# Weights in groups of two tiles, and one bank of G masked straight from PSUM, in a fused SSD and ReGLU kernel

## The chip, the cores and the metric

The kernel runs on one core of a Trainium2 chip. The metric is the device time of one execution in microseconds (us); of several runs the median is taken. Below, PE is the matrix engine (TensorE), DVE is VectorE, ACT is ScalarE, POOL is GpSimd and SP is the engine that issues most loads.

## What is computed

A state-space layer (SSD, in chunks) is followed by a gated feed-forward layer over the same tokens. Cut to what matters:

```python
# x: 4 x 8 x 768 x 32, a: 4 x 8 x 768, B and C: 4 x 8 x 768 x 16; for each chunk:
    L = np.exp(cum[:, :, :, None] - cum[:, :, None, :]) * causal
    CB = np.einsum('bhin,bhjn->bhij', Cc, Bc)
    y_intra = np.einsum('bhij,bhjd->bhid', CB * L, xc)
    y_inter = np.einsum('bhin,bhnd->bhid', Cc, state) * decay_to_i[:, :, :, None]
    y[:, :, sl] = y_intra + y_inter
    state = decay_full[:, :, None, None] * state + np.sum(Bx, axis=2)
# then, with the heads put side by side: 3072 tokens x 256
    gate = np.maximum(x @ w_gate, 0.0)      # w_gate, w_val: 256 x 1536
    val = x @ w_val
    return gate * val @ w_out               # w_out: 1536 x 256
```

## The kernel before

**Tiling.** The state-space layer goes over pairs of 128 positions: 12 pairs of 256 tokens, three for each of four batches. The feed-forward layer goes over six blocks of 512 tokens (two pairs each). Its inner width of 1536 is cut into 12 tiles of 128, called f. For each f, a gate and a value product are formed in PSUM (`gv` for 512 tokens, lines 589 to 601; `gvh` for one pair of 256, lines 603 to 623), ScalarE applies the ReLU, VectorE multiplies, and the result lies in `h` in SBUF. When all 12 tiles of a block are there, `fout` (line 625) multiplies `h` by `wo`, 12 matmuls for each 128 tokens.

**Weights.** `wg`, `wv` and `wo` hold the three weight matrices in bf16 for the whole run. The inputs are in float32, and GpSimd's DMA queue casts them on the way (`weights`, line 186, and `weights_out`, line 192). One `weights(f0, f1)` is two DMAs, one for `wg` and one for `wv`, each of 256 rows. `weights_out` is one DMA of 12 x 128 rows. All of them go through one queue (q0 in the profile) in the order in which GpSimd issues them, and GpSimd also computes between them. The loads of x, B and C are issued by SP (q1), the first few by ScalarE too (q10).

**One pair in the first batch.** For pairs 0 to 2, B and C are scaled by running products of `a` (`scale_wide`, line 269; factors in `wfac`), transposed by TensorE (`turn`, line 657, k=1 for C and k=0 for B) and copied out of PSUM with a mask (`tevac`, line 323). `G_wide` (line 365) forms the products of B and C in four PSUM banks, q = 0 to 3. Each bank is brought to SBUF as bf16 (`gs`) and masked causally. This is done in one of two ways: `gcopy` (line 387) copies with ScalarE and `gmask` (line 381) then masks in SBUF; or `gmask(..., True)` reads PSUM and masks in the same instruction. `adds` (line 397) forms the state's increments from the scaled B and the cast x (`cast_x`, line 299); `carry` and `pass_on` (lines 420 and 431) run the state on; `inter_wide` and `D_wide` (lines 438 and 454) form y; `yevac_wide` (line 468) writes it to `yT`, which the feed-forward layer reads. `decay` (line 240) forms factors for the later batches from `cp` and `pick`; `pick` is finished by GpSimd in `middle` (line 234), once VectorE has `rmid`.

**Order.** The order on each engine is that of the program text: `in_order` (line 15) chains the instructions of each engine as they were written. The start of the kernel (lines 663 to 800) is written out by hand; the loop from line 802 on does the remaining blocks. `keep_warm(n)` issues n matmuls whose result nobody reads. PSUM tiles called `bank` share five banks in turn, so a product waits until the fifth one before it has been read. The raw loads have four buffers in turn.

**Around the change.** Before it issues the first weights, GpSimd copies one element of `wfac` into a small tile `gate` (line 668), so that the weights' transfers begin only after VectorE has made `wfac` (line 667). Then come `weights(0, 2)` and `weights(2, 6)`, the scaling of pair 1 in four instructions (lines 680 and 681, printed at L277 in the profile), the cast of pair 1 (line 682), `pick`, `weights(6, NF)`, the mask of bank 1 of pair 1 (line 727) and `weights_out` (line 728), and then the scaling of pair 2 (lines 742 and 743).

Of the kernel before, what the change touches and what calls it, by code (L numbers as in the profile page):

```python
# [8 lines left out]
FP32 = mybir.dt.float32  # L9
# [20 lines left out]
def kernel(  # L30
# [13 lines left out]
    nc = tc.nc  # L44
# [7 lines left out]
    NF = DF // 128  # L52
# [4 lines left out]
    const = ctx.enter_context(tc.tile_pool(name="const", bufs=1))  # L57
# [8 lines left out]
    def bank(name="bank", shape=(128, 512), dtype=FP32):  # L66
        return mm.tile(list(shape), dtype, tag="shared", bufs=NSHARED, name=name)
# [109 lines left out]
    def keep_warm(n, rhs=warm):  # L177
        w = bank("w", (128, 128))
        for _ in range(n):
            nc.tensor.matmul(out=w, lhsT=warm, rhs=rhs, start=True, stop=True)  # L180

    wg = glob.tile([128, 2, DF], BF16)
    wv = glob.tile([128, 2, DF], BF16)
    wo = glob.tile([128, NF, DM], BF16)

    def weights(f0, f1):
        fs = slice(f0 * 128, f1 * 128)
        for w, src in ((wg, moe_w_gate), (wv, moe_w_val)):
            nc.gpsimd.dma_start(
                out=w[:, :, fs], in_=src[:, fs].rearrange("(k p) f -> p k f", k=2))  # L190

    def weights_out(f0, f1):
        nc.gpsimd.dma_start(
            out=wo[:, f0:f1, :],
            in_=moe_w_out[f0 * 128:f1 * 128, :].rearrange("(o i) m -> i o m", i=128))

    gate = const.tile([1, 2], FP32)

# [1 line left out]
    wfac = glob.tile([128, 2, 2, NH, PPB], FP32)  # L202
# [37 lines left out]
    def decay():  # L240

        d = mm.tile([128, HC, 2, NB, 8], FP32, tag="tp", name="dec")
        for k in range(HC):
            nc.tensor.matmul(
                out=d[:, k].rearrange("p w b h -> p (w b h)"),
                lhsT=cp[:, k * 128:(k + 1) * 128],
                rhs=pick.rearrange("p w h -> p (w h)"),
                start=(k == 0), stop=True, skip_group_check=True)
        st["dec"] = d
# [19 lines left out]
    def scale_wide(p, j, eng):  # L269
        s = st[p]  # L270
        if "bs" not in s:
            s["bs"] = bs = att.tile([128, 4, 128], BF16, tag="bs", name="bs")
            s["tin"] = [[bs[:, 2 * j + r] for r in range(2)] for j in range(2)]
        src = s["bcr"].rearrange("s (t q) j r n -> s j r t q n", t=2)[:, j]
        f = wfac[:, j, :, :, p]
        for t in range(2):
            eng.tensor_tensor(  # L277
                out=s["bs"][:, 2 * j:2 * j + 2].rearrange(
                    "s k (q t n) -> s k t q n", q=4, t=2)[:, :, t],
                in0=src[:, :, t],  # L280
                in1=f[:, :, 4 * t:4 * t + 4].to_broadcast([128, 2, 4, N]),
                op=ALU.mult)
# [16 lines left out]
    def cast_x(p, ceng):  # L299
        s = st[p]  # L300
        cast = ceng.copy if ceng is nc.scalar else ceng.tensor_copy
        xb = att.tile([128, 2 * NH * D], BF16, tag="xb", name="xb")
        if p < NWIDE:
            cast(xb, s["xr"].rearrange("s h r d -> s (h r d)"))
            s["xb"] = xb.rearrange("s (h r d) -> s h r d", h=NH, r=2)
        else:
            cast(xb, s["xr"].rearrange("s i h d -> s (i h d)"))
            s["x"] = [xb[:, i * NH * D:(i + 1) * NH * D] for i in range(2)]
# [56 lines left out]
    def G_wide(p):  # L365
        s = st[p]
        g = [bank("g%d" % q, (128, 2, 2, 128)) for q in range(4)]
        for r in range(2):
            for i in range(2):
                for q in range(4):  # L370
                    rows = slice(32 * q, 32 * q + 32)
                    nc.tensor.matmul(  # L372
                        out=g[q][64 * i:64 * i + 64, r],
                        lhsT=s["BT"][rows, r, 64 * i:64 * i + 64], rhs=s["CT"][rows, :, i],
                        start=(r == 0), stop=True, tile_position=(32 * q, 64 * i),
                        skip_group_check=True)
        s["gp"] = g
        s["gs"] = att.tile([128, 4, 4, 128], BF16, tag="gs", name="gs", bufs=2)
        s["gw"] = s["gs"].rearrange("s q (r t) m -> s q r t m", r=2)

    def gmask(p, q, eng, psum=False):
        s = st[p]
        d = s["gw"][:, q]
        m = wmask.unsqueeze(2).to_broadcast([128, 2, 2, 128])
        eng.tensor_tensor(out=d, in0=s["gp"][q] if psum else d, in1=m, op=ALU.mult)  # L385

    def gcopy(p, q):
        s = st[p]
        nc.scalar.copy(out=s["gw"][:, q], in_=s["gp"][q])  # L389

    def y_wide(p):
        s = st[p]
        if "yw" not in s:
            s["yw"] = [mm.tile([128, 512], FP32, tag=t, name=t) for t in ("y", "Aps")]
            s["begun"] = [False, False]

    def adds(p):
        y_wide(p)
        s = st[p]
        s["A"] = [s["yw"][i][:, 256:320] for i in range(2)]  # L400
        if p == 0:
            s["A"][0] = bank("A0", (128, 2 * D))
        halves = [i for i in range(2) if 2 * p + i < NC - 1]
        for r in range(2):
            for i in halves:
                half = slice(64 * i, 64 * i + 64)
                for q in range(4):
                    nc.tensor.matmul(
                        out=s["A"][i][32 * q:32 * q + 32],
                        lhsT=s["bs"][half, r, 32 * q:32 * q + 32],  # L410
                        rhs=s["xb"].rearrange("s (t q) r d -> s q r t d", t=2)[half, q, r],
                        start=r == 0, stop=True,
                        tile_position=(64 * i, 32 * q), skip_group_check=True)
        for i in halves:
            s["begun"][i] = p > 0 or i > 0
# [4 lines left out]
    def carry(p, i):  # L420

        c = 2 * p + i
        T_[c] = n = att.tile([128, 2 * D], FP32, tag="T", name="T", bufs=3)
        if c == 0:
            nc.scalar.copy(out=n, in_=st[p]["A"][i])
        else:
            nc.vector.scalar_tensor_tensor(
                out=n, in0=T_.pop(c - 1), scalar=dec[:, c - 1:c], in1=st[p]["A"][i],
                op0=ALU.mult, op1=ALU.add)

    def pass_on(p, i):

        c = 2 * p + i
        S[c + 1] = m = att.tile([128, 2, D], BF16, tag="Sw", name="Sw", bufs=3)
        src = st[p]["A"][i] if c == 0 else T_[c]
        nc.scalar.mul(m.rearrange("s t d -> s (t d)"), src, dec[:, c:c + 1])
# [166 lines left out]
    def gvh(b, f, u, later=False):  # L603

        if f == 0 and u == 0:
            fst[b] = ffn.tile([128, NF, 512], BF16, tag="h", name="h")
        tk = slice(b * 512 + u * 256, b * 512 + (u + 1) * 256)
        fs = slice(f * 128, (f + 1) * 128)
        gv_ = bank("gv", (128, 2, 256))
        for j, w in ((0, wg), (1, wv)):  # L610
            for k in range(2):
                nc.tensor.matmul(out=gv_[:, j], lhsT=w[:, k, fs], rhs=yT[:, k, tk],  # L612
                                 start=(k == 0), stop=(k == 1), skip_group_check=True)
        r = ffn.tile([128, 512], BF16, tag="r", name="r", bufs=5)[:, 0:256]
        nc.scalar.activation(r, gv_[:, 0], AF.Relu)  # L615

        def finish():
            nc.vector.tensor_tensor(out=fst[b][:, f, u * 256:(u + 1) * 256], in0=r,  # L618
                                    in1=gv_[:, 1], op=ALU.mult)

        if later:
            return finish
        finish()
# [37 lines left out]
    V, A_, P_ = nc.vector, nc.scalar, nc.gpsimd  # L661
# [3 lines left out]
    decays(0)  # L665
    keep_warm(8)
    nc.vector.tensor_copy(wfac[:, 1], d)
    nc.gpsimd.tensor_copy(gate[:, 0:1], wfac[0:1, 1, 0, 0, 0:1])
    weights(0, 2)
    weights(2, 6)  # L670
    scale_wide(0, 1, V)
    nc.vector.reciprocal(wfac[:, 0, :, :, 0], wfac[:, 1, :, :, 0])
    scale_wide(0, 0, V)
# [5 lines left out]
    scan(0, H)  # L679
    scale_wide(1, 1, P_)  # L680
    scale_wide(1, 0, P_)
    cast_x(1, P_)
    keep_warm(6)
    G_wide(0)
    keep_warm(7)
# [3 lines left out]
    cast_x(0, A_)  # L689
    decays(1)  # L690
    adds(0)
    gcopy(0, 1)
    gmask(0, 3, V, True)
    keep_warm(4, st[0]["gw"][:, 3, 0, 0])
    gmask(0, 0, V)
    gmask(0, 1, V)
    pass_on(0, 0)
    carry(0, 0)
    middle()
# [6 lines left out]
    load(2)  # L706
    load(3)
    carry(0, 1)
    weights(6, NF)
    tevac(1, V, A_)  # L710
    pass_on(0, 1)
    def halves(b, u, *fs):
# [2 lines left out]

    f0 = gvh(0, 0, 0, True)
    G_wide(1)
    adds(1)
    decay()
    gcopy(1, 0)  # L720
    gmask(1, 2, V, True)
    f0()
# [1 line left out]
    gmask(1, 3, V, True)  # L724
    carry(1, 0)
    pass_on(1, 0)
    gmask(1, 1, P_)
    weights_out(0, NF)
    gmask(1, 0, V)
    late = [gvh(0, f, 0, True) for f in (1, 2, 3)]  # L730
    inter_wide(1)
    D_wide(1)
# [169 lines left out]
```

## Time and profile before

| | |
|---|---|
| median of 5 runs | 128.39 us (127.72 to 129.1) |
| profiled execution | 128.29 us |
| its span, first to last instruction | 126.5 us |
| TensorE matmuls busy | 119.4 us, 94% of the span |
| VectorE, ScalarE, GpSimd busy | 88.4, 81.8 and 42.3 us |
| DMA | 12.15 MB, mean 96 GB/s |
| GpSimd's queue q0 | 3184 packets, 2.36 MB |
| SP's queue q1 | 66096 packets, 8.91 MB |
| `wg` and `wv`, tiles 0 to 1: issue to landing | 5.0 and 4.5 us |
| tiles 2 to 5 | 5.2 and 7.0 us |
| tiles 6 to 11 | 6.7 and 8.0 us |
| `wo` | 11.3 us |
| matmul with 256 or 512 columns | 273 or 379 ns |
| mask from PSUM on VectorE (L385) | 629 to 692 ns |
| mask from SBUF on VectorE (L385) | 426 to 867 ns |
| mask from SBUF on GpSimd (L385) | 1150 to 1156 ns |

Times in the profile are counted from the start of the span. An engine's row gives its start, its duration, and in brackets how long the engine had been idle before and what ended the wait. A weight DMA's "issue" is GpSimd's own time for it, 0.7 to 1.1 us; the transfer runs afterwards, and "to landing" counts from the beginning of the issue until the semaphore says that the data is there.

### The profile page before, as it was taken

The numbers are of one execution on the slowest core, as the hardware profiler recorded it, in microseconds if no ns is written. First come the engines' busy times: TensorE is split into PE (matmuls) and PEld (weight loads), VectorE is DVE, ScalarE is ACT, GpSimd is POOL, SyncE is SP. The second block draws the span as 40 slices with busy tenths as digits, with TensorE's granted clock in tenths as the row PEclk, the third lists the DMA queues.
The fourth block names the chain that finished last, engine by engine and source line by source line (L and its number), as shares of the span: only waits on it lengthen the run. The fifth ranks groups of instructions, "written<-read, shape, count | busy, mean of one in ns | idle before, by whom it ended". The sixth has DMA issues, their size and how long they took to land.

```text
span 126.5 us, 3627 instructions
## 1 busy us (share of the span) xinstructions
PE 119.4 (94%) x1382; PEld 83.5 (66%) x1388; DVE 88.4 (70%) x196; ACT 81.8 (65%) x184; POOL 42.3 (33%) x86
## 2 busy tenths in 40 slices
PE   6979798999999999999999999999999999999980
PEld 6856583378776478875477865577864678844770
DVE  4795887755799675998674898664989656788420
ACT  0478587845688843787936787845987646877310
POOL 6589807418345016802312803232600033000000
PEclk9999999999999999999999999999999999999998
DMA  4999999976997988597922399802200002200031
GB/s 66 210 178 201 173 212 199 123 97 81 113 111 208 112 101 97 152 145 88 108 39 88 89 115 111 105 8 83 88 0 0 0 0 88 83 0 0 5 120 46
DMA packets 72209, 12.15 MB, mean 96 GB/s; under 512 B 65936, under 2 KB 72192, under 8 KB 72192
## 3 DMA queue, kind: packets, MB, share of 16 engines
q1 hardware_dynamic: 66096, 8.91, 46.3%
q0 software_dynamic: 3184, 2.36, 12.5%
q10 hardware_dynamic: 2912, 0.66, 2.5%
q8 instruction: 11, 0.18, 0.6%
q14 instruction: 6, 0.05, 0.2%
HBM read 11.13 MB, written 3.15 MB: 113 GB/s over the span
## 4 chain that ended last, share of the span: by engine, by line
PE 83%; DMA 9%; DVE 2%; ACT 2%; POOL 1%; issue 1%; DVEq 0%; POOLq 0%
PE o L630 26%; PE gv L612 16%; PE val L597 14%; PE gate L594 12%; DMA wo<-in_moe_w_out_dram 9%; PE w L180 3%; PE y L569 2%; PE g L481 2%; PE tp L321 2%; PE y L558 1%; ACT gs L389 1%; PE g L372 1%; POOL gs L385 1%; PE A_ps L528 1%; DVE bs L277 1%
## 5 line engine op out<-in xcount | busy, mean ns | idle before, releaser
L601 DVE TENSOR_TENSOR h<-r,val 128x512 bf16<-128x512 bf16 x44 | 29.5, 686 | 9.2 <-ACT r L600 7.0
L630 PE MATMUL o<-wo,h 128*128 128x256 bf16 x288 | 34.2, 273 | 0.4 <-DMA wo<-in_moe_w_out_dram 0.4
L630 PEld LDWEIGHTS <-h 128*128 128x128 bf16 x288 | 27.1, 98 | 5.6 <-issue 1.5
L600 ACT ACTIVATE r<-gate 128x512 bf16<-128x512 f32 x44 | 25.9, 600 | 6.5 <-PE gate L594 4.5
L597 PE MATMUL val<-yT,wv 128*128 128x512 bf16 x88 | 26.2, 379 | 0.8 <-DMA wv<-in_moe_w_val_dram 0.5
L594 PE MATMUL gate<-yT,wg 128*128 128x512 bf16 x82 | 24.9, 379 | 0.0
L618 DVE TENSOR_TENSOR h<-r,gv 128x256 bf16<-128x256 bf16 x56 | 22.5, 418 | 2.7 <-ACT r L615 1.8
L615 ACT ACTIVATE r<-gv 128x256 bf16<-128x256 f32 x56 | 21.4, 385 | 2.5 <-PE gv L612 0.5
L612 PE MATMUL gv<-yT,wv 128*128 128x256 bf16 x112 | 21.4, 273 | 0.7 <-DMA wv<-in_moe_w_val_dram 0.7
L612 PE MATMUL gv<-yT,wg 128*128 128x256 bf16 x112 | 21.5, 273 | 0.1
L489 POOL TENSOR_SCALAR_AFFINE_SELECT gs<-gs 128x512 bf16<-128x512 bf16 (+1 forms) x18 | 9.0, 523 | 33.0 <-ACT gs L500 33.0
L506 DVE TENSOR_TENSOR gs<-g,maskUT 128x512 bf16<-128x512 f32 x18 | 11.6, 686 | 11.7 <-issue 9.6
L291 POOL TENSOR_TENSOR bs<-bcr,scaleBC 128x256 bf16<-128x256 f32 x18 | 11.0, 633 | 20.0 <-PE val L597 5.8
L597 PEld LDWEIGHTS <-wv 128*128 128x128 bf16 x88 | 8.5, 98 | 10.9 <-DMA wv<-in_moe_w_val_dram 0.8
L594 PEld LDWEIGHTS <-wg 128*128 128x128 bf16 x88 | 8.2, 98 | 7.0
L612 PEld LDWEIGHTS <-wv 128*128 128x128 bf16 x112 | 10.9, 98 | 2.2 <-DMA wv<-in_moe_w_val_dram 0.9
L612 PEld LDWEIGHTS <-wg 128*128 128x128 bf16 x112 | 10.2, 98 | 2.0 <-issue 0.2
L500 ACT CAST gs<-g 128x512 bf16<-128x512 f32 x9 | 5.3, 589 | 6.7 <-PE g L481 6.7
L582 ACT CAST yT<-y 128x512 bf16<-128x512 f32 x9 | 5.3, 586 | 5.3 <-PE y L569 2.7
L652 ACT COPY ob<-o 128x512 f32<-128x512 f32 x9 | 5.3, 584 | 4.1 <-PE o L630 4.1
L180 PE MATMUL w<-warm 128*128 128x128 bf16 x49 | 5.6, 288 | 1.1 <-DVE tmask L154 1.1
L180 PEld LDWEIGHTS <-warm 128*128 128x128 bf16 x58 | 5.2, 129 | 1.6 <-DVE tmask L154 1.0
(103 smaller groups left out, 118.3 us busy)
## 6 DMA issues: line engine op xcount, KB each, us to landing
out_dram<-ob SPq DMA_DIRECT2D x10, 256.0 KB, 2.2
xr<-in_x_dram SPq DMA_DIRECT2D x19, 128.0 KB, 3.6
bcr<-in_C_dram SPq DMA_DIRECT2D x19, 64.0 KB, 3.4
bcr<-in_B_dram SPq DMA_DIRECT2D x19, 64.0 KB, 3.6
wo<-in_moe_w_out_dram POOLq DMA_DIRECT2D x1, 768.0 KB, 11.3
xr<-in_x_dram SPq DMA_DIRECT2D x2, 256.0 KB, 8.5
wg<-in_moe_w_gate_dram POOLq DMA_DIRECT2D x1, 384.0 KB, 6.7
wv<-in_moe_w_val_dram POOLq DMA_DIRECT2D x1, 384.0 KB, 8.0
```

The lines of the kernel that those rows point to most:

```text
L180: nc.tensor.matmul(out=w, lhsT=warm, rhs=rhs, start=True, stop=True)
L291: eng.tensor_tensor(out=bs.rearrange("s k (q t n) -> s k t q n", q=4, t=2)[:, :, t], in0=src[:, :, t], in1=f[:, :, 4 * t:4 * t + 4].to_bro ...
L489: nc.gpsimd.affine_select(out=dst, in_=dst, pattern=[[0, n], [1, 128]], compare_op=ALU.is_ge, fill=0.0, base=0, channel_multiplier=-1)
L506: nc.vector.tensor_tensor(out=d[:, q], in0=g[q], in1=m, op=ALU.mult)
L594: nc.tensor.matmul(out=g, lhsT=wg[:, k, fs], rhs=yT[:, k, tk], start=(k == 0), stop=(k == 1))
L597: nc.tensor.matmul(out=v, lhsT=wv[:, k, fs], rhs=yT[:, k, tk], start=(k == 0), stop=(k == 1))
L600: nc.scalar.activation(r, g, AF.Relu)
L601: nc.vector.tensor_tensor(out=fst[b][:, f], in0=r, in1=v, op=ALU.mult)
L612: nc.tensor.matmul(out=gv_[:, j], lhsT=w[:, k, fs], rhs=yT[:, k, tk], start=(k == 0), stop=(k == 1), skip_group_check=True)
L615: nc.scalar.activation(r, gv_[:, 0], AF.Relu)
L618: nc.vector.tensor_tensor(out=fst[b][:, f, u * 256:(u + 1) * 256], in0=r, in1=gv_[:, 1], op=ALU.mult)
L630: nc.tensor.matmul(out=o[:, ts % 2], lhsT=fst[b][:, f, ts * 128:(ts + 1) * 128], rhs=wo[:, f], start=(f == 0), stop=(f == NF - 1), skip_gr ...
```

## The change

`weights` takes a third argument, so that `wg` and `wv` of a group can be issued apart. The weights are issued in groups: tiles 0-1, 2-3, `wg` of 4-5; then pair 1 is scaled; then `wv` of 4-5, `pick`, the cast of pair 1, tiles 6-7, tiles 8-11 and `wo`. The tile `gate` and GpSimd's copy are gone; VectorE sets one element of `wg` to zero after it has made `wfac`, and the first weight DMA waits for that, since it overwrites it. Bank 1 of pair 0 is no longer copied by ScalarE and then masked: VectorE masks it from PSUM. Bank 1 of pair 1 is masked by VectorE after bank 0, no longer by GpSimd. `decay` comes ahead of `adds(1)` on TensorE. The whole diff:

```diff
-    def weights(f0, f1):
+    def weights(f0, f1, which=(0, 1)):
         fs = slice(f0 * 128, f1 * 128)
-        for w, src in ((wg, moe_w_gate), (wv, moe_w_val)):
+        for j in which:
+            w, src = ((wg, moe_w_gate), (wv, moe_w_val))[j]
             nc.gpsimd.dma_start(
                 out=w[:, :, fs], in_=src[:, fs].rearrange("(k p) f -> p k f", k=2))
...
-    gate = const.tile([1, 2], FP32)
...
     nc.vector.tensor_copy(wfac[:, 1], d)
-    nc.gpsimd.tensor_copy(gate[:, 0:1], wfac[0:1, 1, 0, 0, 0:1])
+    nc.vector.memset(wg[0:1, 0, 0:1], 0.0)
     weights(0, 2)
-    weights(2, 6)
+    weights(2, 4)
+    weights(4, 6, (0,))
     scale_wide(0, 1, V)
...
     scale_wide(1, 1, P_)
     scale_wide(1, 0, P_)
-    cast_x(1, P_)
+    weights(4, 6, (1,))
     keep_warm(6)
...
     adds(0)
-    gcopy(0, 1)
     gmask(0, 3, V, True)
     keep_warm(4, st[0]["gw"][:, 3, 0, 0])
     gmask(0, 0, V)
-    gmask(0, 1, V)
+    gmask(0, 1, V, True)
     pass_on(0, 0)
...
     carry(0, 1)
-    weights(6, NF)
+    cast_x(1, P_)
+    weights(6, 8)
+    weights(8, NF)
+    weights_out(0, NF)
     tevac(1, V, A_)
...
     G_wide(1)
+    decay()
     adds(1)
-    decay()
     gcopy(1, 0)
...
     pass_on(1, 0)
-    gmask(1, 1, P_)
-    weights_out(0, NF)
     gmask(1, 0, V)
+    gmask(1, 1, V)
     late = [gvh(0, f, 0, True) for f in (1, 2, 3)]
```

## The prediction, made before the changed kernel was run

> **What bounds the kernel now.** First the page's chain of work that ended last, by engine; then that chain in order of time; then the waits of the first 55 us. The page:
>
> ```profile
> PE 83%; DMA 9%; DVE 2%; ACT 2%; POOL 1%; issue 1%; DVEq 0%; POOLq 0%
> ```
>
> TensorE is the bound, and from 25.44 us on it runs without a gap worth naming. So the change can only act through the moment at which that unbroken stretch begins. The chain in order of time shows the moment:
>
> ```profile
> 11.74 1.07 ACT gs L389 x2
> 12.85 0.10 issue
> 12.96 1.10 POOL gs L385
> 14.06 11.33 DMA wo<-in_moe_w_out_dram
> 25.39 0.05 issue
> 25.44 1.48 PE o L630 x12
> ```
>
> The stretch begins with `fout(0, 0)` at 25.44, when `wo` has landed at 25.39. The waits show three stalls of TensorE on weights:
>
> ```profile
> PE gv L612 <- DMA wv<-in_moe_w_val_dram: 0.7, 1, 0.7
> ...
> PE val L597 <- DMA wv<-in_moe_w_val_dram: 0.5, 1, 0.5
> ...
> PE o L630 <- DMA wo<-in_moe_w_out_dram: 0.4, 1, 0.4
> ```
>
> The timeline puts them at 14.10 (0.66 us, `wv` tiles 2 to 5), 19.93 (0.51, `wv` tiles 6 to 11) and 25.44 (0.36, `wo`). They stand in a row: whatever is saved at the first two is handed to the third unless `wo` lands earlier. So I looked at the DMA engines, one microsecond at a time (packets, MB, share of the engines). GpSimd's queue q0 in the windows from 9, 10 and 12 us, each from its own answer:
>
> ```profile
> q0 software_dynamic: 309, 0.20, 136.1%
> ```
>
> ```profile
> q0 software_dynamic: 207, 0.20, 121.5%
> ```
>
> ```profile
> q0 software_dynamic: 29, 0.02, 14.5%
> ```
>
> SP's queue q1 and q0 from 21 us, and the busy share of the engines in the 40 slices of the window from 24 us:
>
> ```profile
> q0 software_dynamic: 329, 0.17, 121.3%
> q1 hardware_dynamic: 327, 0.03, 51.6%
> ```
>
> ```profile
> DMA  4544444464443434553444344466687999999899
> ```
>
> From 9 and from 10 us q0 moves equal bytes in packets of different sizes; from 12 us it is nearly dry. While `wo` moves, SP's loads of later pairs take one packet for each of its packets. At 24 us the share has fallen to four tenths: most engines have run out, a few lag, and `wo` counts as landed with the last of them. The timeline of GpSimd, which issues all weights:
>
> ```profile
> 7.07 0.72 POOL L189 DMA_DIRECT2D wv<-in_moe_w_val_dram  x1
> 8.23 1.94 POOL L277 TENSOR_TENSOR bs<-bcr,wfac 128x128 bf16<-128x128 f32 x4 [0.45 <-DMA bcr<-in_C_dram]
> ...
> 14.06 1.07 POOL L193 DMA_DIRECT2D wo<-in_moe_w_out_dram  x1
> ```
>
> **What the Trainium skill says.** "DMA: Bandwidth & Descriptors", section "Queues, rings and completion order": each DMA engine goes round-robin between the queues that have work, packet by packet. The trace agrees: 329 packets against 327. Same page, "Latency and other measured facts": about 1 us to the first byte of a GpSimd DMA. Here it is longer: `wg` tiles 6 to 11 are issued at 11.05, and in the window 12 to 13 us q0 still moves only 29 packets; I use 2 us. Same page, "Why small descriptors are slow (HBM only)": a fixed overhead per packet. The trace's packet records agree: 512 B took 60 ns, 1024 B 98, 1536 B 135, so about 22 ns are fixed. "SBUF — State Buffer", section "Who interferes with whom": a VectorE tensor_tensor with two SBUF inputs contends with GpSimd's reads. Agrees: the SBUF mask at 13.52 took 0.87 us beside GpSimd's own mask, others 0.43 to 0.54.
>
> **The change, part by part.**
>
> *GpSimd's start.* Its 0.30 us copy (L668) goes; a 0.06 us VectorE memset after `wfac` (4.39) takes its place, delaying VectorE's scaling by about 0.05. The first DMA starts near 4.5 instead of 4.71.
>
> *Five issues ahead of pair 1's scaling instead of four.* 4.5 + 0.93 + 4 x 0.72 = 8.3; the scaling started at 8.23 because it waited 0.45 us for a load. So +0.08 us, and its end moves from 10.17 to 10.25. The `tpb` transposes of pair 1 started at 10.26 right behind it: TensorE +0.05 to 0.08. Without that 0.45 us of cover the fifth issue would cost 0.5.
>
> *After the scaling.* `wv` 4-5: 0.79 to 11.05; `pick` 0.35 to 11.4; cast of pair 1 0.6 to 12.0; four issues 0.79 + 3 x 0.72 to 14.9; `wo` 1.07 to 15.95. So `wo` is issued 0.85 us later, although GpSimd lost its 1.15 us mask. Who needs these: `decay` (now first) needs `pick` at about 11.7: there. `adds(1)` needs the cast after decay's 0.88, at 12.5: there; in the old order it would have waited 0.3. Pair 2's scaling starts 0.8 later, but its second half waited for a load to 19.52 anyway, and `turn(2)` comes after 20.9. As built, the last three weight DMAs wait for the landing of the first three weight DMAs, which they follow on the same semaphores; these land by about 11, before 13.4: nothing.
>
> *Pair 0's bank.* ScalarE loses a 0.59 copy, so its `Sw` goes from 8.96 to about 8.65; VectorE's mask reads PSUM, 0.63 instead of 0.43. D's last quarter is ready at 9.65 rather than 9.54. Net -0.1 us at most, hidden behind the `tpb` transposes that wait for GpSimd. Nothing.
>
> *Pair 1's mask on VectorE.* VectorE is free for masks at 13.52; two at 0.43 to 0.54 end at 14.5, two at 0.87 at 15.3. TensorE, without its 0.66 stall, wants `D_wide(1)` at 15.19 - 0.66 + 0.05 = 14.6. GpSimd only issues DMAs then, so I take the short value: no wait (else +0.7, again ahead of `wo`).
>
> *The weights.* At 0.20 MB per us (windows 9 to 10 and 10 to 11 us) from 8 us on, tiles 2-3 (0.5 MB in total) land by about 11.2; used at 13. `wv` 4-5 moves from about 12.3 to 13.5; used at 15.1. Tiles 6-7 are issued from 12.0, so data from 14 to 15.5; used at 18.4. Tiles 8-11 by about 19.5 with laggards; used at 20.1 and 20.5. Both `wv` stalls go: -0.66 - 0.51.
>
> *Sum at `fout(0, 0)`.* TensorE was ready at 25.44 - 0.36 = 25.08; now 25.08 - 0.66 - 0.51 + 0.05 = about 23.95 (24.65 with slow masks). The stall goes to `wo`.
>
> *When does `wo` land?* The same bytes in the same queue. Before, q0 ran nearly dry from 12 to 13 us (29 packets), about 0.8 us lost; after, it is starved by late issue for about as long, around 11.5 to 12 and 13 to 14. The start is up to 0.2 earlier. The regrouping makes four more DMAs of 256 rows, so 1024 more packets (6 x 256 + 1536 of `wo` = 3072 become 4096), 64 more per engine. Lower bound of their cost: nothing, since the queue moved 0.20 MB both from 9 to 10 (309 packets) and from 10 to 11 us (207). Upper bound: 64 x 22 ns = 1.4 us, and more where each draws a q1 packet in. I take 0.3: 25.4 - 0.2 + 0.3 - 0.1 = 25.4, between 24 and 26.5.
>
> The span is then 126.5 + (25.4 - 25.4) = 126.5, the profiled execution 128.29, 0.1 under the median of 128.39. Forecast 128.4: the stall of 0.36 grows to about 1.4, and nothing is won.
>
> **Rivals.**
>
> *`wo` lands early (faster).* If no engine lags, it ends near 23.7, where most engines stopped in the packet records; TensorE starts at 23.95 to 24.5. Worth up to 25.4 - 24 = 1.4 us. For it: GpSimd's pauses let laggards catch up. Against it: they lagged at each weight DMA since 13 us. A cap: pair 3's last C load is issued at 25.47 and takes 2.8 us, to 28.3; its scaling began at 29.10, so beyond 0.8 us the gain meets this. 127.4.
>
> *Each new packet costs (slower).* 64 more packets per engine at 22 ns, each drawing a q1 packet of 0.516 x 16 us / 327 = 25 ns: 3.0 us at most, half of it likely if the laggards are always full: +1.5, 129.9. It decides as soon as `wo` lands after 25.4. For it: one-for-one at 21 us. Against: the equal bytes at 9 and 10 us.
>
> *`wo` follows its issue (slower).* As the chain draws it, GpSimd's issue leads to the landing; issued 0.85 later, it lands 0.85 later: 129.2. Against: 11.3 us for 0.75 MB, twice what 0.20 MB per us would need, so it queued.
>
> **How the numbers follow.** No change, with `wo` within 0.5 us of before: 0.5. Early `wo`: 0.2, of which half passes 1%. Packet cost: 0.15, most of it beyond 1%. Issue-bound: 0.15, mostly within 1%. About 1% (1.3 us) is what a measurement of this kernel can tell from no change. So faster 0.12, same 0.74, slower 0.14. The range leaves out the outer half of both tails: 127.2 to 129.7; the likeliest case alone spans 127.9 to 128.9.
>
> **What would show it.** Right: no `wv` wait on TensorE, one `wo` wait of 1 to 2 us at L630, which starts near 25.4. Wrong: a start under 24.6 or over 26.3; a `wv` wait that stays; TensorE waiting for the pair 1 cast at L408; D_wide(1) after 15; `turn(2)` or `turn(3)` waiting for GpSimd.

## The result, and the profile after

The changed kernel takes 128.99 us (median of 44 runs, 128.16 to 130.35); the kernel before takes 128.26 us in the 79 runs beside it. The ratio is 1.005, with a 95% interval of 1.0037 to 1.0063: slower by about 0.6 us, inside the 1% that the prediction called no change. The profiled execution took 129.38 us with a span of 127.5 us, against 128.29 and 126.5 before. The ratios leave out executions more than 1.5% above the fastest of their kernel (8 of 19 in a_join, 5 of 22 in b_68_early, at most 4 in any other); the medians keep them.

The page's chain by engine shows the same bound as before, with more GpSimd in it:

```profile
PE 83%; DMA 9%; POOL 3%; DVE 1%; ACT 1%; issue 1%; DVEq 0%; ACTq 0%
```

The chain in order of time, in the window from 12 us (start, duration, what):

```profile
11.95 0.72 POOL wg L190
...
12.67 0.72 POOL wv L190
13.38 0.71 POOL wg L190
14.10 0.66 POOL wv L190
14.75 0.05 issue
14.80 11.60 DMA wo<-in_moe_w_out_dram
26.41 0.05 issue
26.45 1.48 PE o L630 x12
```

The unbroken stretch of TensorE begins at L630 at 26.45 instead of 25.44, again on the landing of `wo`. That is 1.01 us later, and the span is 1.0 us longer: what follows L630 is unchanged. A single pair of profiles overstates the medians' difference (0.73 us) a little; the executions of one kernel differ by more than that.

The waits of the first 55 us, those of TensorE on weights (total, times, longest):

```profile
PE o L630 <- DMA wo<-in_moe_w_out_dram: 0.9, 1, 0.9
...
PE val L597 <- DMA wv<-in_moe_w_val_dram: 0.7, 1, 0.7
PE gate L594 <- DMA wg<-in_moe_w_gate_dram: 0.5, 1, 0.5
```

TensorE's timeline places them:

```profile
20.83 0.60 PE L594 MATMUL gate<-yT,wg 128*128 128x512 bf16 x2 [0.50 <-DMA wg<-in_moe_w_gate_dram]
22.09 0.61 PE L597 MATMUL val<-yT,wv 128*128 128x512 bf16 x2 [0.66 <-DMA wv<-in_moe_w_val_dram]
...
26.45 1.48 PE L630 MATMUL o<-wo,h 128*128 128x256 bf16 x12 [0.94 <-DMA wo<-in_moe_w_out_dram]
```

The two old stalls, 0.66 at tile 2 and 0.51 at tile 6, are gone. Two new ones of 0.50 and 0.66 us stand at tile 8, the head of the last group. So 1.17 us were won and 1.16 us given back before TensorE even came to `wo`, and then the stall on `wo` grew from 0.36 to 0.94.

GpSimd's timeline:

```profile
4.72 0.93 POOL L190 DMA_DIRECT2D wg<-in_moe_w_gate_dram  x1 [1.77 <-DVE bs L277]
...
8.54 1.71 POOL L277 TENSOR_TENSOR bs<-bcr,wfac 128x128 bf16<-128x128 f32 x4
...
11.90 0.77 POOL L190 DMA_DIRECT2D wg<-in_moe_w_gate_dram  x1
...
14.09 0.72 POOL L190 DMA_DIRECT2D wv<-in_moe_w_val_dram  x1
14.80 1.03 POOL L194 DMA_DIRECT2D wo<-in_moe_w_out_dram  x1
```

From the scaling of pair 1 on, the issues come within 0.1 us of where the prediction put them. The DMA engines do not do what it said. In the window of one microsecond from 16 us on (packets, MB, share of the engines), first the kernel before:

```profile
q0 software_dynamic: 126, 0.19, 110.9%
q1 hardware_dynamic: 35, 0.00, 3.4%
```

and the changed kernel:

```profile
q1 hardware_dynamic: 643, 0.15, 81.0%
q0 software_dynamic: 148, 0.07, 50.7%
```

In the same microsecond, the weights' queue q0 moved 0.19 MB before and 0.07 MB after, while SP's loads in q1 went from next to nothing to 0.15 MB. Summed over the packet records, q0 had brought 1498 KB by 18 us before and 1113 KB after. It catches up later (1925 against 1672 KB by 21 us), but not in time for tile 8, which waits, nor wholly for `wo`.

### The profile page after: what moved, and what is told of

It reads as the page before. It is cut to its first block, busy times and chain, and to the rows that moved or that the text cites. A ratio compares the mean times of both kernels' runs of the same rounds, so it can differ in the third digit from the quotient of the medians.

```text
span 127.5 us, 3628 instructions
## 1 busy us (share of the span) xinstructions
PE 120.0 (94%) x1382; PEld 83.9 (66%) x1388; DVE 88.7 (70%) x198; ACT 81.3 (64%) x183; POOL 43.4 (34%) x88
## 4 chain that ended last, share of the span: by engine, by line
PE 83%; DMA 9%; POOL 3%; DVE 1%; ACT 1%; issue 1%; DVEq 0%; ACTq 0%
PE o L630 26%; PE gv L612 16%; PE val L597 13%; PE gate L594 12%; DMA wo<-in_moe_w_out_dram 9%; PE w L180 4%; PE y L569 2%; PE g L481 2%; PE tp L321 2%; PE y L558 1%; POOL wg L190 1%; POOL wv L190 1%; PE A_ps L528 1%; PE g L372 1%; PE y L462 1%
## 5 line engine op out<-in xcount | busy, mean ns | idle before, releaser
L601 DVE TENSOR_TENSOR h<-r,val 128x512 bf16<-128x512 bf16 x44 | 29.5, 686 | 10.2 <-ACT r L600 7.4
L630 PE MATMUL o<-wo,h 128*128 128x256 bf16 x288 | 34.2, 273 | 0.9 <-DMA wo<-in_moe_w_out_dram 0.9
L630 PEld LDWEIGHTS <-h 128*128 128x128 bf16 x288 | 27.1, 98 | 6.2 <-issue 1.5
L615 ACT ACTIVATE r<-gv 128x256 bf16<-128x256 f32 x56 | 21.2, 385 | 2.1
L612 PEld LDWEIGHTS <-wg 128*128 128x128 bf16 x112 | 10.2, 98 | 2.0 <-issue 0.3
L385 DVE TENSOR_TENSOR gs<-g,wmask 128x512 bf16<-128x512 f32 x7 | 4.7, 678 | 2.9 <-PE g L372 2.9
```

Source lines behind the costliest of these rows:

```text
L601: nc.vector.tensor_tensor(out=fst[b][:, f], in0=r, in1=v, op=ALU.mult)
L630: nc.tensor.matmul(out=o[:, ts % 2], lhsT=fst[b][:, f, ts * 128:(ts + 1) * 128], rhs=wo[:, f], start=(f == 0), stop=(f == NF - 1), skip_gr ...
```

## The experiments

Of a run with a new label, the letters "a" and "b" say which kernel it starts from: the changed one or the one before. The theories that the expectations weigh (where one uses a letter, its own words say what it stands for):

- **Supply:** the weights reach q0 in small late portions, the queue has too little in it between 11.5 and 17 us, and SP's loads take the engines.
- **Packets:** the 1024 additional packets cost time by their number.
- **The rest of the change:** masks, memset, `decay`.
- **Own issue:** `wo` lands a fixed time after its own issue; against it, that `wo` lands when the bytes ahead of it in the queue are through.

All results first. "Landed" and "L630" (its first start in TensorE's timeline) are from the profiled execution; the last column is the span less the start of L630.

| run | ratio to before, 95% interval | `wo` issued, landed | L630 | span | rest |
|---|---|---|---|---|---|
| before | 1 | 14.06, 25.39 | 25.44 | 126.5 | 101.1 |
| after | 1.005 [1.0037, 1.0063] | 14.80, 26.41 | 26.45 | 127.5 | 101.1 |
| a_old_groups | 1.0003 [0.9979, 1.0028] | 12.06, 24.48 | 24.53 | 125.6 | 101.1 |
| a_join | 1.011 [1.0074, 1.0146] | 13.36, 25.46 | 27.93 | 129.0 | 101.1 |
| a_early | 1.0435 [1.0379, 1.0491] | 12.06, 23.86 | 31.86 | 133.0 | 101.1 |
| a_loads_late | 1.0489 [1.0444, 1.0535] | 14.78, 26.18 | 31.78 | 133.1 | 101.3 |
| b_wo_late | 1.0007 [0.9984, 1.0029] | 15.27, 25.57 | 25.65 | 126.7 | 101.1 |
| b_split6 | 1.0043 [1.002, 1.0067] | 14.93, 26.41 | 26.46 | 127.6 | 101.1 |
| a_old_split | 0.998 [0.9955, 1.0005] | two DMAs | 24.70 | 125.8 | 101.1 |
| a_old_load3 | 1.0 [0.9973, 1.0026] | 12.06, 24.56 | 26.59 | 127.7 | 101.1 |
| b_68_early | 0.9964 [0.9939, 0.9989] | 14.56, 24.8 | 24.85 | 126.0 | 101.1 |
| b_wo_split | 0.9971 [0.9949, 0.9993] | two DMAs | 24.23 | 125.3 | 101.1 |
| a_68_early | 0.9961 [0.9939, 0.9983] | 13.12, 24.97 | 25.01 | 126.1 | 101.1 |
| a_best | 0.9936 [0.9906, 0.9967] | two DMAs | 24.17 | 125.3 | 101.1 |

The last column is the firmest finding: over 14 kernels it is 101.1 us, once 101.3. Whatever is done to the weights acts only through the start of L630.

The columns from `wo` on come from one execution each. In the 43 executions of the kernel before that ran beside b_68_early, the span goes from 125.9 to 127.4 us, so some tenths in a landing say little; between kernels the ratios decide.

**a_old_groups**: the changed kernel with the old groups; masks, memset and `decay` stay changed.

```diff
-    weights(2, 4)
-    weights(4, 6, (0,))
+    weights(2, 6)
...
-    weights(4, 6, (1,))
...
-    weights(6, 8)
-    weights(8, NF)
+    weights(6, NF)
```

> The changed kernel with the weights in the groups and places of before (tiles 0-1 and 2-5 ahead of pair 1's scaling, 6-11 and wo behind it, after pick and the cast); masks, memset, and decay before adds stay as changed. Theory A, late issue: what costs is that GpSimd hands the queue its weights in small portions and late, so the queue runs dry from 11.5 to 15 us and SP's loads take the engines. Then wo lands at 25.4 or earlier again, and the time is that of before, within 0.3 us. Theory B, packets: the 1024 extra packets cost. Same expectation here. Theory C, not the weights but the masks, decay or the memset: the time stays 0.5 us or more above before. The wv stalls of 0.66 and 0.51 us come back in A and B.

Measured 128.44 us, 1.0003: level with before. `wo` was issued at 12.06 and landed at 24.48. So the masks, the memset and `decay` together cost nothing that can be measured, and the loss lies in the weights' groups and places. The profiled execution (127.54 us) was one of this kernel's fastest; the two `wv` stalls that were expected back do not show in it.

**a_join**: the changed kernel with tiles 6 to 11 in one group at its new place.

```diff
-    weights(6, 8)
-    weights(8, NF)
+    weights(6, NF)
```

> The changed kernel with tiles 6 to 11 in one group behind the cast instead of 6-7 and 8-11: two issues fewer, 512 packets fewer, wo issued at 13.4 instead of 14.8 us. Theory A, late issue: the first data of 6 to 11 come no earlier than in the changed kernel, so TensorE waits for them longer at tile 6, but wo follows sooner: it lands 0.3 to 0.8 us earlier than 26.4. Theory B, packets: half of the extra packets are gone, so half of the 1.0 us delay of wo, 25.9. The time stays between before and the changed kernel.

Measured 1.011: worse, where the joined group was to bring the time between the two kernels. `wo` did land earlier, at 25.46. But the group's `wv` lands only at 21.2, and it now covers tile 6, which is used earlier than tile 8. Its TensorE waits there 0.33 and then 2.11 us; the windows of 5 us after that (engines' busy time, then PEclk, DMA share, GB/s):

```profile
20.00:25.00 5.00, 3.74 (x10) 1.39 (x11) 1.48 (x3) 0.99 (x3) 0.61 (x1) 0.66 1.72 196
25.00:30.00 5.00, 5.00 (x56) 2.87 (x54) 2.95 (x6) 3.41 (x8) 0.00 (x0) 1.00 0.85 99
```

The granted clock falls to 0.66 in the stretch with the wait. L630 starts at 27.93 although `wo` had landed at 25.46. Without its stalls at tile 8 the changed kernel's TensorE would have been ready near 24.35 (25.51 less 1.16); with the 2.44 us of waits here that makes about 26.8, an estimate, so about 1.1 us more went with the lower clock. A late weight can thus cost more than its wait. This was one execution of 130.99 us; the ratio is the safer reading of the kernel.

**a_early**: all weights, in the small groups, and `wo` ahead of pair 1's scaling.

```diff
-    weights(4, 6, (0,))
+    weights(4, 6)
+    weights(6, 8)
+    weights(8, NF)
+    weights_out(0, NF)
...
-    weights(4, 6, (1,))
...
-    weights(6, 8)
-    weights(8, NF)
-    weights_out(0, NF)
```

> The changed kernel with its own small groups and its 4096 packets, but all of them and wo issued ahead of pair 1's scaling, without a pause (wo issued near 12.1 us). Pair 1's scaling begins some 4.6 us later, so TensorE is late in pair 1 and the time itself is no measure, about 1 to 4 us above before; what counts is wo's landing. Theory A, late issue: the queue never runs dry, so wo lands at 24 us or earlier. Theory B, packets: the number and size of packets is that of the changed kernel, so wo lands at 26 us or later.

`wo` was issued at 12.06, as in a_old_groups, with the same 4096 packets as the changed kernel. It landed at 23.86, where the packets theory asked for 26 or later, and 0.6 us before that of a_old_groups with its 3072. The number of packets alone is not what costs. The kernel as a whole is 4% slower, for another reason, shown by TensorE's timeline:

```profile
13.99 0.39 PE L321 MATMUL tp<-ident,bs 128*128 128x128 bf16 x2 [4.07 <-POOL bs L277]
```

and by its windows:

```profile
10.00:15.00 5.00, 0.68 (x5) 0.42 (x6) 0.62 (x3) 0.92 (x3) 5.00 (x10) 0.86 1.27 161
15.00:20.00 5.00, 5.00 (x54) 3.42 (x52) 2.98 (x8) 2.69 (x7) 1.52 (x4) 0.50 1.55 207
```

TensorE waits 4.07 us for GpSimd's scaling behind the issues, and the clock is 0.50 for the next 5 us.

**a_loads_late**: the changed kernel with SP's loads of pairs 2 and 3 issued behind `yevac_wide(1)`.

```diff
     yevac_wide(0, A_, V)
-    load(2)
-    load(3)
     carry(0, 1)
...
     yevac_wide(1, A_, V)
+    load(2)
+    load(3)
```

> The changed kernel with SP's loads of pairs 2 and 3 held back from 10.8 us to about 15.5 us (behind yevac_wide(1)). Theory A with the loads as takers: in the changed kernel SP's loads moved about 0.27 MB from 14.5 to 17 us while the weights crept; held back, the weights get the engines, tiles 8-11 land before TensorE asks (no stall at tile 8), and wo lands about 1 us earlier, near 25.4. If the loads only fill time that the weights cannot use, wo stays at 26.4. Pair 2's transposes may then wait for their B load, a new stall of up to 1 us. Theory B, packets: wo stays within 0.3 of 26.4.

Tiles 8 to 11 landed at 19.36 and 20.66, 1.4 us earlier, and their wait shrank to 0.32. So it was indeed SP's loads that had held them up. But `wo` landed at 26.18 and not at 25.4: the loads, now later, ran beside `wo` instead. And GpSimd's scaling of pair 2 waited for them:

```profile
22.62 0.78 POOL L277 TENSOR_TENSOR bs<-bcr,wfac 128x128 bf16<-128x128 f32 x2 [6.81 <-DMA bcr<-in_C_dram]
25.64 0.78 POOL L277 TENSOR_TENSOR bs<-bcr,wfac 128x128 bf16<-128x128 f32 x2 [2.24 <-DMA bcr<-in_B_dram]
```

TensorE waited 2.17 and 2.73 us in its turn, and the clock fell to 0.54 in the window from 25 to 30 us. The loads and the weights share the engines; moving one only moves the loss.

**b_wo_late**: the kernel before with `weights_out(0, NF)` behind the first half of pair 2's scaling.

```diff
-    weights_out(0, NF)
...
     scale_wide(2, 1, P_)
+    weights_out(0, NF)
     scale_wide(2, 0, P_)
```

> The kernel before with one thing changed: wo is issued behind the first half of pair 2's scaling, at about 16 us instead of 14.06, so 1.9 us later; the weights ahead of it keep their groups and issue times. Theory Q, the queue: what matters is that the queue has work, and tiles 6-11 keep it busy to about 18 us, so wo lands at 25.4 as before (within 0.4 us) and the time is that of before. Theory I, its own issue: wo lands a fixed 11 to 12 us behind its own issue, so at 27.3, and the time is about 1.5 to 2 us (1.3%) above before.

`wo` was issued at 15.27, 1.2 us later than before, and landed at 25.57, 0.2 us later:

```profile
wo<-in_moe_w_out_dram POOLq DMA_DIRECT2D x1, 768.0 KB, 10.3
```

The time is the same (1.0007 [0.9984, 1.0029]). The landing does not follow its own issue; `wo` queued.

**b_split6**: the kernel before with one edit of the change.

```diff
-    weights(6, NF)
+    weights(6, 8)
+    weights(8, NF)
```

> The kernel before with one thing changed: tiles 6-11 are issued as 6-7 and 8-11, two issues more between 11 and 14 us, so wo's issue moves by about 1.4 us to 15.5. Theory Q, the queue: the first portion is 0.25 MB instead of 0.75 and is followed 1.4 us later by the rest, which the queue reaches about in time, so tiles 8-11 and wo move by less than 0.5 us and the time by less than 0.3%. Theory I, own issue: wo lands 1.4 us later, at 26.8, time about 1% above before. Theory B, packets: 512 packets more, half of the changed kernel's extra, wo 0.5 us later.

Measured 1.0043, L630 at 26.46: this one split costs about as much as the whole change. None of the three theories had its size: the queue theory asked for less than 0.3% and less than 0.5 us at `wo`, the packets for 0.5 us, the own issue for 1.4. Its chain:

```profile
14.93 11.48 DMA wo<-in_moe_w_out_dram
26.46 1.48 PE o L630 x12
```

The issue of `wo` moved by 0.87 us; b_wo_late says that this alone costs 0.2. What differs is what q0 moves in the meantime: with packets of 512 and 1024 bytes instead of 1536 it moves, from 14 us on, 199 packets and 0.10 MB in a microsecond, beside 805 packets of q1; before, 110 packets and 0.17 MB beside 154. By 21 us it had brought 1751 KB against 1925.

**a_old_load3**: a_old_groups with pair 3's loads issued ahead of pair 4's, behind a one-element memset that holds them back from 13.8 to 17.7 us.

```diff
+        if p == 3:
+            nc.vector.memset(bcr[0:1, 0, 0, 0, 0:1], 0.0)
...
-    load(3)
...
     decay_factors()
+    load(3)
     load(4)
```

> The changed kernel with the groups and places of before, and SP's loads of pair 3 held back from about 14 to 17 us (behind a VectorE write after the second-last of pair 1's finishes). In the kernels before it q1 gave one packet for each packet of wo. If q1's packets are what delays wo, it lands 0.5 to 1 us earlier (near 23.7) and the time falls 0.3 to 0.6% below before, unless pair 3's scaling waits for its loads at 28 us. If q1 only fills room that wo leaves, nothing changes (1.000 of before).

Measured 1.0; `wo` landed at 24.56, as in a_old_groups. This does not clear q1, because the loads were moved into the transfer of `wo` and not out of it. From 18 to 21 us the two queues took turns in both kernels: in each microsecond 237 to 240 packets of q0 beside 236 to 239 of q1 in a_old_groups, 252 to 258 beside 251 to 253 here, and q0 moved 0.12 to 0.14 MB where it moved 0.20 in b_68_early from 21 us with 22 packets of q1 beside it. What q1 costs `wo` was not isolated. In this profile other loads were late (a `wv` wait of 0.92, pair 2's transposes 1.83), which moved its L630.

**a_old_split**: a_old_groups with `wo` in two DMAs.

```diff
-    weights_out(0, NF)
+    weights_out(0, 6)
+    weights_out(6, NF)
```

> The changed kernel with the groups and places of before, and wo in two DMAs, tiles 0-5 and 6-11. TensorE needs the second half 0.66 us after the first. If wo's landing sets the start of the unbroken stretch (Theories A, Q and I alike), the first half lands 1.5 to 2.5 us ahead of the whole, TensorE's stall there shrinks to the 0 to 0.5 us by which the second half is late, and the time falls 0.3 to 0.6% below before. If wo is not what binds, no change against the same kernel with one DMA (1.000 of before).

Measured 0.998 [0.9955, 1.0005]; no wait on `wo` is left, but 0.41 and 0.80 us on `wv`. Not clearly faster than before, where 0.3 to 0.6% was expected.

**b_68_early**: b_split6 with tiles 6 and 7 ahead of pair 1's scaling; packets as in b_split6.

```diff
     weights(2, 6)
+    weights(6, 8)
...
-    weights(6, NF)
+    weights(8, NF)
```

> The kernel before with tiles 6 and 7 cut off from 6 to 11, as in b_split6, but issued ahead of pair 1's scaling, right behind tiles 2 to 5; tiles 8 to 11 stay where 6 to 11 were. Same packets and same moment of the issue of wo (14.9) as in b_split6; what differs is that GpSimd's queue has work while GpSimd scales pair 1. Theory that the queue is left short of work from 11.5 to 17 us: it stays full then, wo lands at 25.4 or earlier, although it is issued at 14.9. Theory that taking turns with SP's loads by 512-byte packets costs the time: wo lands near 26.4 as in b_split6. In both, pair 1's scaling starts about 1.4 us later (9.7), less the 0.45 us that it waited, so TensorE waits about 1 us longer at pair 1's transposes and is ready for the output product no earlier than about 25.4: the time is 128.3 to 129.0 by the first, 129.2 or more by the second.

Measured 127.97 us, 0.9964 [0.9939, 0.9989]: faster than before by about as much as b_split6 is slower, and faster than either theory had asked. `wo` landed 10.2 us after its issue at 14.56, at 24.8, which is 1.6 us earlier than in b_split6 with the issue only 0.4 earlier. TensorE no longer waited for it; the chain in order of time runs through ReLU and product of the last tile instead:

```profile
23.54 0.61 ACT r L600
...
24.17 0.70 DVE h L601
24.87 1.47 PE o L630 x12
```

The same bytes in the same packets landed earlier, so neither number nor size of the packets decides by itself: the place of the group ahead of the scaling does. That it acts through the queue's supply is argued from the bytes below. One part of the expectation missed: the queue did not stay full. From 14 us on:

```profile
q1 hardware_dynamic: 1067, 0.13, 112.1%
q0 software_dynamic: 62, 0.06, 34.2%
```

q0 is short there too, but by then it has brought its bytes: by the packet records 1026 KB by 14.5 us against 911 in b_split6. The lead of 115 KB grows to 196 by 21 us (1947 against 1751), worth about 1.0 us at 0.20 MB per us; the other 0.6 us of the earlier landing it leaves open. TensorE also waited only 0.39 us for the later scaling at its `tpb` transposes, and not 1 us.

**b_wo_split**: the kernel before with `wo` in two DMAs (the edit of a_old_split).

> The kernel before with wo in two DMAs, tiles 0 to 5 and 6 to 11. The output product's first six matmuls need only the first half. Theory that the landing of wo sets the start of the unbroken stretch: the first half lands before TensorE is ready at 25.1, the wait of 0.36 us goes, L630 starts near 25.1 and the time falls by 0.3 to 0.4 us, to a ratio of 0.997. Rival, that the second issue of about 0.9 us delays pair 2 or that the halves land together: no change, ratio 1.000.

Measured 127.96 us, 0.9971 [0.9949, 0.9993]. L630 started at 24.23 with no wait; part of that is that this execution showed no `wv` stall either. The first matmuls need only the first half, so part of the wait is bought off for one more issue of about 0.65 us.

**a_68_early** and **a_best**: the changed kernel with tiles 2 to 5 in one group and tiles 6 and 7 ahead of the scaling; a_best has `wo` in two DMAs besides.

```diff
-    weights(2, 4)
-    weights(4, 6, (0,))
+    weights(2, 6)
+    weights(6, 8)
...
-    weights(4, 6, (1,))
...
-    weights(6, 8)
...
-    weights_out(0, NF)
+    weights_out(0, 6)
+    weights_out(6, NF)
```

> The changed kernel with tiles 2 to 5 as one group again and tiles 6 and 7 issued ahead of pair 1's scaling; tiles 8 to 11 and wo stay where the change put them, and so do the masks, the memset and decay. Theory that the change's cost is the queue left short of work from 11.5 to 17 us: with tiles 6 and 7 in the queue wo lands by about 24.8 as in b_68_early, no wait on weights of over 0.4 us is left, L630 starts near 24.9, and the time is 127.8 to 128.2, a ratio near 0.997 to before and 0.992 to the changed kernel. Rival, that something else of the change (masks, decay, memset beside the small groups) costs: 128.8 or more.

> As a_68_early, with wo in two DMAs, tiles 0 to 5 and 6 to 11. If wo's landing still sets the start of L630 there, the split gains up to 0.4 us on it; if TensorE's own work and the ReLU of the last tile set it, as the chain of b_68_early has it, the split gives nothing: the same within 0.2 us. I expect the second, 127.9.

a_68_early took 127.82 us, 0.9961 [0.9939, 0.9983]; a wait of 0.6 us on `wo`, landed at 24.97, was left, 0.2 more than expected. a_best took 127.54 us, 0.9936 [0.9906, 0.9967]. By the two ratios it is 1.1% below the changed kernel (0.9936 / 1.005 = 0.989). Against the expectation, L630 started 0.84 us earlier than in a_68_early. TensorE's timeline:

```profile
23.74 0.59 PE L597 MATMUL val<-yT,wv 128*128 128x512 bf16 x2
24.17 1.04 PE L630 MATMUL o<-wo,h 128*128 128x256 bf16 x8
```

TensorE comes to L630 straight from the last tile, with no idle time before it (none is given in brackets). The intervals of a_68_early and a_best overlap, so the split's own share is not settled; that a_best beats both kernels is.

## Why the prediction was right, and where it was wrong

It was right that nothing would be won, and about where the time is decided: at the landing of `wo`. By the signs that it named itself, its working was wrong. L630 began at 26.45, beyond its limit of 26.3; a `wv` wait stands, of 0.66 us, though at another tile; and the wait on `wo`, 0.94, is below its 1 to 2 us. Forecast 128.4 and measured 128.99 agree to 0.5% because the loss of a microsecond that it had wrong is small beside 128, which is luck as far as the weights go. Its steps in order:

- **GpSimd's start** near 4.5: wrong, 4.72 as before. The wait behind which it starts is named as VectorE's scaling, the instruction after the memset. The data came earlier all the same, and by more than the 0.2 us credited: q0's first packet starts at 7.01 instead of 7.92, and by 8 us q0 had brought 130 KB instead of 2. The other four kernels with GpSimd's copy had 3 to 9 KB by then, the other eight with the memset 100 to 148; why is open. By 12 us the lead was gone (645 against 744 KB), because the 640 KB issued ahead of the scaling were through.
- **Issues, scaling, later issues:** the scaling ended at 10.25 as worked out, `wo` was issued at 14.80 (14.9 forecast), and `adds(1)` did not wait.
- **Masks and D:** the two SBUF masks of pair 1 ended at 14.51 (14.5), 0.76 us for both; D of pair 1 started at 14.58 (14.6). "SBUF — State Buffer" of the Trainium skill, section "Who interferes with whom", says that GpSimd's reads contend with such a VectorE operation; GpSimd was only issuing DMAs then, and the short value held.
- **Weights:** both old stalls went. The step that failed is "Tiles 8-11 by about 19.5 with laggards". They landed at 20.8 and 22.1. It let q0 run at 0.20 MB per us from about 2 us behind an issue on, so that tiles 6-7 moved from 14 to 15.5 and tiles 8-11 right behind them; the windows from 14, 15 and 16 us show 0.09, 0.09 and 0.07 MB.
- **TensorE ready** at 23.95: it was 25.51 (26.45 - 0.94). Of the 1.56 us, 1.16 are the stalls at tile 8. Another 0.2 to 0.3 stem from the front: `G_wide(0)`'s copy began at 7.32 instead of 7.00. a_join and a_loads_late, with the same instructions up to there, did not show that, so it belongs to the execution.
- **`wo` lands** at 25.4: 26.41, by the same failed term. The sum set the queue's shortage after the change equal to that before ("starved by late issue for about as long"), 0.8 us. The records show q0 385 KB behind at 18 us, which is 1.9 us at 0.20 MB per us; at the landing of `wo` 1.0 us was left. The step's upper end of 26.5 held it.
- **Rivals.** The packet rival asked for 129.9 and was refuted by a_early and b_68_early. "`wo` follows its issue" gave 129.2, close to the measured time, by a mechanism that b_wo_late refutes: there 1.2 us of later issue made 0.2. Early landing did not come about. One-for-one turns, which the prediction took from 21 us, held there again (about 350 packets of each queue per microsecond).

What was missed, then, is a coupling between the queues and not an instruction. The prediction costed the small groups by what they add to GpSimd's time and to the packets. It did not ask who uses the engines while the queue is short. SP's loads of the next pairs were waiting, and took them: GpSimd's scaling of pair 2 got its last load at 17.74 instead of 19.52 us, and TensorE paid for it with the waits at tile 8.

What stays open: in the microseconds from 13 to 15 of b_split6 the engines are full (78% by q0 and 44% by q1 in the first of them). There q0 may lose to turns with q1 as much as to its own short supply, and no run separates the two within that stretch. Nor does late issue cover the whole loss of the changed kernel. Of the 385 KB by 18 us, 226 were missing by 16 us and 159 more came in the two microseconds after, when every weight had been issued (`wo` at 14.80). In those two q1 moved 1078 packets beside 251 of q0, which is not one for one, and a burst of the kind meets the kernel before too, from 18 to 19 us (559 beside 135). What sets q1's share there is not shown. The same groups with larger packets were not tried.

## What to carry to other kernels

Where a transfer queues behind others, as `wo` does here, cost a regrouping by the cumulative bytes of its queue against the need, not by the issue time of the last one. Smaller groups helped the first user here, but the queue did not stay ahead; ask what other queue stands ready to fill the gap, and put the small group ahead of the issuer's pause and not behind it. When stalls stand in a row, look for the next user of each resource: here about as much stall as was removed appeared two tiles further on (1.16 against 1.17 us; so close a match in one execution is chance).

## What the runs showed of the hardware

- **The clock after waits.** The clock was half for 3.41 us in a_join (from 21.41), for 6.83 in a_loads_late (from 25.36) and for 10.24 in a_early (from 13.57): once, twice and three times the same length. In the 3.41 us before each of these moments, TensorE's matmuls had been busy for 0.98, 0.28 and 0.00 us. "TensorE: Matmul & The Clock Gate" of the Trainium skill, Part 1, "What's actually happening", has the clock at half after an idle window of about 3.4 us. The third case, with its wait of 4.07 us, agrees; in a_join a longest wait of 2.11 us was enough, with nearly a microsecond of work in the same 3.41 us. In a_old_load3 a stretch of the same length with 1.89 us of work (22.36 to 25.77, counted back from that run's own change of clock) kept the full clock.
- **Issue to data.** The first packet of GpSimd's queue started 7.01 us into the span for an issue at 4.72, and 7.92 before for one at 4.71: 2.3 and 3.2 us, above the 2 us that the prediction used.
- **A landing's last part.** In b_68_early 2294 of q0's 2304 KB are there by 23.5 us; the last 10 take until 24.3, and `wo` counts as landed at 24.8. That fits a few engines which end late, but the records do not name a packet's engine.
- **The price of a turn goes by the other queue's packet.** From 21 us q0 moved 385 packets of 512 bytes in a microsecond in b_68_early, with 22 of q1 beside them. In the changed kernel, from 21 to 24 us, it moved 349 to 358 beside as many of q1 with 64 bytes each; in a_old_groups, from 18 to 21 us, 237 to 240 beside as many of q1 with 256 bytes each. One turn given away for each turn taken thus took less than a tenth of the rate in the one case and 0.4 in the other.
